# Seven half products for the last expert's first layer, set between the steps of two other experts

## The chip, the cores and the metric

The kernel runs on one core of a Trainium2 chip. The metric is the device time of one execution in microseconds (us). Executions of this kernel mostly agree within 0.3%, so a difference of 1 us in 385 is just within reach if a kernel is run five or six times. The profile also gives the span from the first to the last instruction, mostly 1.6 to 2.0 us shorter than the device time, and the mean granted clock of TensorE (1.0 is full speed).

I write PE for TensorE's matmuls, PEld for its weight loads, DVE for VectorE, ACT for ScalarE, POOL for GpSimd, SP for the engine whose queue issues most transfers. L12 is line 12 of the kernel that ran; a line has another number in another kernel. A bank is one of the buffers of 128x512 f32 in PSUM that a step of matmuls fills and ScalarE or VectorE empties.

## The reference

Attention over 4 batches of 768 positions and 8 heads makes the rows x. A mixture of four experts follows, and it is the part that matters here:

```python
# N, D, E, F = 3072, 512, 4, 1024
p = domain_probs / (domain_probs.sum(-1, keepdims=True) + 1e-09)
out = np.zeros((N, D))
for e in range(E):
    h = np.maximum(x @ w1[e], 0.0)          # first layer
    out += p[:, e:e + 1] * (h @ w2[e])      # second layer
```

## The kernel before

The first four tiles of 128 tokens are computed plainly: three together in a stage of "units", then one in a single-tile stage. The other twenty go in ten pairs. For a pair, each expert's inputs are scaled by its probability on VectorE (`scale_inputs`), the first layer is 32 matmuls over 256 columns (two tiles) per expert, and ScalarE evicts them with a Relu into blocks of `hA`. The second layer is already a Winograd-Strassen product: seven half products in place of eight, for which VectorE makes sums of the blocks (S1 to S4) and, once, sums of the weights (`tsb`).

```python
    blocks = hA.rearrange("p (b k x) -> p b k x", b=6, k=KT)
    A11, A21, A12, A22, S1, S2 = (blocks[:, n, :, :] for n in range(6))
    S3, S4 = A21, A12
    # ... cut ...
    def scale_inputs(nt0, e):
        xs = xs_of[0][:, e % 2, :, :]                    # two slots
        # ... out=o (xs), in0=x, in1=probabilities, on VectorE ...

    def input_sums(k0, k1):                              # VectorE
        # S1 = A21 + A22, S3 = A11 - A21, S2 = S1 - A11, for k0..k1

    def pair_steps(nt0, nxt):
        sums = [lambda: last_weight_sum(E - 1)] if nt0 == pair0 else []
        for e in range(E):
            if e + 1 < E:
                scale_inputs(nt0, e + 1)
            # ... load_probs(nxt) with the last expert ...
            for f0 in range(0, FTP, 2):                  # 4 steps of 8 matmuls
                # 8 matmuls of 256 columns -> one bank; Relu by ScalarE -> hA
                if sums:
                    sums.pop(0)()                        # one sum behind each step
                yield 2 * DMP * mm_ns(PC), 0.5
            # ... sums += input_sums(...) ...
        for op in sums:
            op()
        o = moe.tile([P, PT, DM], FP32, name="o", bufs=1)        # the outputs
        s = moe.tile([P, 3, HN], FP32, name="s", tag="sums", bufs=1)
        # ... seven products x, y in turn; store(0) after the sixth, store(1) after the seventh ...

    def moe_steps():
        # ... units ...
        for e in range(E):                               # the single tile
            yield from plain_steps(3, 1, e, ...)
            if e + 1 < E:
                last_weight_sum(e)
            if e == E - 3:
                scale_inputs(pairs[0], 0)
        for n, nt0 in enumerate(pairs):
            yield from pair_steps(nt0, ...)
```

Between the steps (at each `yield`) pieces of the attention of later chunks are put in, so every engine's queue mixes the two. The order in each queue is fixed when the kernel is built.

The softmax here doesn't subtract the row's maximum and nothing guards it: scores larger than these inputs give would overflow.

## Time and profile before

| | before |
|---|---|
| time, median of 3 | 384.93 us (384.45 to 385.48) |
| span of the profiled run, clock | 382.6 us, 0.999 |
| PE / DVE / ACT busy | 374.2 / 235.5 / 233.6 us |

The page gives busy time per engine over the span, then 40 slices of the span with the busy share in tenths. The view of stretches gives the same for any window. A busy share is an average, while a wait is decided by the one thing that comes last. And PE's idle time is counted from the modelled end of the last matmul, some 0.16 us after the next could have started (a matmul over 256 columns is given 272 ns, where one follows the other after 109), so short waits do not show at all and longer ones look a little too short.

### The profile page before, as it was taken

To read this page: it belongs to the slowest core of one execution; us is meant where nothing else is said; L and a number is where in the kernel's file an instruction comes from. 1 tells how busy PE (TensorE), PEld (TensorE's weight loads), DVE (VectorE), ACT (ScalarE), POOL (GpSimd) and SP (SyncE) were. 2 spreads that over 40 slices of the span, in tenths; PEclk is the share of its full clock that TensorE was granted. 3 is DMA by queue.
4 is the path that set the end of the run, shared out by engine and by line. 5 is a ranking of instruction groups with operands and counts; after the bars stand their busy time and mean duration, and the time that the engine had idled before them with its cause. 6 is when DMAs were issued, how large, how long until landed. Compare 5 with 4: busy or idle time off the path is not lost.

```text
span 382.6 us, 9369 instructions
## 1 busy us (share of the span) xinstructions
PE 374.2 (98%) x3814; PEld 312.2 (82%) x3814; DVE 235.5 (62%) x516; ACT 233.6 (61%) x476; POOL 111.7 (29%) x152
## 2 busy tenths in 40 slices
PE   8989999999999999999999999999999999999996
PEld 4755556577998898999888998899888999888885
DVE  7745787577866757766547567775556565345440
ACT  3863567657786876765765784674765684551630
POOL 8933644855138028113800118212100000000000
PEclk9999999999999999999999999999999999999999
DMA  9999999999499959974940759965510210110001
GB/s 165 150 207 201 185 174 193 149 159 177 67 139 130 123 101 96 143 134 50 138 72 20 123 102 82 151 123 38 81 55 15 67 57 2 57 56 30 29 0 57
DMA packets 127192, 39.19 MB, mean 102 GB/s; under 512 B 116232, under 2 KB 120876, under 8 KB 127148
## 3 DMA queue, kind: packets, MB, share of 16 engines
q0 software_dynamic: 86816, 19.01, 58.1%
q1 hardware_dynamic: 38732, 19.18, 22.3%
q8 instruction: 30, 0.49, 0.5%
q10 hardware_dynamic: 1600, 0.39, 0.5%
q14 instruction: 14, 0.11, 0.1%
HBM read 44.88 MB, written 6.34 MB: 134 GB/s over the span
## 4 chain that ended last, share of the span: by engine, by line
PE 86%; DMA 7%; POOL 3%; DVE 2%; ACT 1%; issue 0%; POOLq 0%; ACTq 0%
PE pA L1077 36%; PE pO L1110 32%; DMA w2sb<-in_moe_w_dram 7%; PE pO L986 5%; PE pA L639 5%; PE pA L965 4%; PE pV L687 2%; PE pV L751 2%; POOL vS L297 1%; ACT es L657 1%; POOL vR L291 1%; DVE kS L277 0%; POOL early L436 0%; DVE hA L1002 0%; POOL w1sb L322 0%
## 5 line engine op out<-in xcount | busy, mean ns | idle before, releaser
L1077 PE MATMUL pA<-xs,w1sb 128*128 128x256 f16 x1280 | 148.1, 272 | 0.1
L1077 PEld LDWEIGHTS <-w1sb 128*128 128x128 f16 x1280 | 122.5, 98 | 14.4 <-DVE xs L1043 0.4
L1086 ACT ACTIVATE hA<-pA 128x512 f16<-128x512 f32 x160 | 94.3, 597 | 39.2 <-PE pA L1077 36.7
L1110 PEld LDWEIGHTS <-hA 128*128 128x128 f16 x1120 | 106.6, 98 | 12.9
L657 ACT ACTIVATE es<-pA 128x384 f16<-128x384 f32 (+2 forms) x122 | 59.3, 510 | 32.4 <-PE pA L639 27.8
L1110 PE MATMUL pO<-w2sb,hA 128*128 128x256 f16 x640 | 77.8, 272 | 0.0
L293 POOL DMA_DIRECT2D vS<-in_v_dram x30 | 29.6, 988 | 124.5 <-PE pV L751 123.6
L1043 DVE TENSOR_TENSOR xs<-xT,pB 128x1024 f16<-128x1024 f16 (+1 forms) x52 | 49.6, 973 | 20.0 <-PE pA L1077 19.9
L1110 PE MATMUL pO<-tsb,hA 128*128 128x256 f16 x480 | 58.6, 272 | 0.0
L934 DVE TENSOR_TENSOR hA<-hA 128x1024 f16<-128x1024 f16 (+1 forms) x80 | 42.0, 553 | 1.1
L774 DVE TENSOR_TENSOR xT<-pV,rc 64x384 f16<-64x384 f32 x37 | 20.6, 556 | 25.9 <-ACT rc L779 23.8
L978 ACT ACTIVATE hA<-pA 128x384 f16<-128x384 f32 (+1 forms) x64 | 22.3, 386 | 20.3 <-PE pA L965 17.8
L965 PE MATMUL pA<-xT,w1sb 128*128 128x384 f16 (+1 forms) x256 | 31.7, 273 | 0.1
L986 PE MATMUL pO<-w2sb,hA 128*128 128x512 f16 x128 | 30.5, 379 | 0.3 <-DMA w2sb<-in_moe_w_dram 0.3
L1051 DVE TENSOR_TENSOR hA<-hA 128x512 f16<-128x512 f16 (+1 forms) x30 | 15.3, 512 | 18.8 <-ACT hA L1086 18.5
L769 ACT ACTIVATE rc<-pV,eps 64x384 f32<-64x384 f32 x37 | 21.3, 576 | 8.9 <-PE pV L751 7.7
L965 PEld LDWEIGHTS <-w1sb 128*128 128x128 f16 x256 | 19.3, 98 | 8.4 <-issue 0.5
L1131 DVE TENSOR_TENSOR o<-pO,s 128x256 f32<-128x256 f32 x30 | 12.7, 423 | 20.4 <-PE pO L1110 15.3
L639 PE MATMUL pA<-qT,kR 128*128 128x384 f16 (+2 forms) x120 | 23.3, 278 | 0.6 <-ACT qT L550 0.4
L1128 ACT COPY s<-pO 128x256 f32<-128x256 f32 x30 | 11.2, 373 | 18.1 <-PE pO L1110 17.3
L986 PEld LDWEIGHTS <-hA 128*128 128x128 f16 x128 | 11.9, 98 | 12.2 <-issue 0.5
L291 POOL DMA_DIRECT2D vR<-in_v_dram x24 | 19.0, 811 | 5.5 <-DMA w2sb<-in_moe_w_dram 4.0
(115 smaller groups left out, 331.7 us busy)
## 6 DMA issues: line engine op xcount, KB each, us to landing
pB<-p_rows SPq DMA_DIRECT2D x10, 512.0 KB, 3.6
out_dram<-o SPq DMA_DIRECT2D x19, 256.0 KB, 4.9
w1sb<-in_moe_w_dram POOLq DMA_DIRECT2D x8, 512.0 KB, 10.1
w2sb<-in_moe_w_dram POOLq DMA_DIRECT2D x4, 1024.0 KB, 13.2
vS<-in_v_dram POOLq DMA_DIRECT2D x30, 112.0 KB, 3.5
k_rows<-in_k_dram POOLq DMA_DIRECT2D x18, 128.0 KB, 4.4
q<-in_q_dram POOLq DMA_DIRECT2D x18, 128.0 KB, 5.7
vR<-in_v_dram POOLq DMA_DIRECT2D x24, 48.0 KB, 5.3
```

What stands on the lines that cost most here:

```text
L291: gp.dma_start(out=t[:, :, 0:D], in_=rows_of(v, b, h, c))
L293: gp.dma_start(out=t[:, :, own_v(h)], in_=windows_of(v, b, h, c))
L639: nc.tensor.matmul(out=ps[:, o : o + nq], lhsT=key_tile(b, c, h, t), rhs=qTs[b, c][:, hp, q0 : q0 + nq], start=(n == 0 or not first), stop ...
L657: nc.scalar.activation(out=es[:, 0:cols], in_=ps[:, 0:cols], func=AF.Exp, scale=SC)
L934: nc.vector.tensor_tensor(out=out, in0=a, in1=b, op=ALU.subtract)
L965: nc.tensor.matmul(out=pss[ft][:, 0:cols_n], lhsT=w1sb[:, e * DMP + ct, ft * P : (ft + 1) * P], rhs=x[:, ct, :], start=(n == 0), stop=(n = ...
L978: nc.scalar.activation(out=hs[:, ft, :], in_=ps[:, 0:cols_n], func=AF.Relu)
L986: nc.tensor.matmul(out=ps_o, lhsT=hs[:, ft, j * P : (j + 1) * P], rhs=w2sb[:, e * FTP + ft, :], start=(ft == 0), stop=(ft == FTP - 1),)
L1043: nc.vector.tensor_tensor(out=o, in0=xin, in1=pb.to_broadcast([P, DMP, n, P]), op=ALU.mult)
L1077: nc.tensor.matmul(out=ps[:, f * PC : (f + 1) * PC], lhsT=w1sb[:, e * DMP + ct, (f0 + f) * P : (f0 + f + 1) * P], rhs=xs[:, ct, :], start= ...
L1086: nc.scalar.activation(out=blocks[:, b0 : b0 + 2, k0 : k0 + 2, :].rearrange("p t f x -> p f t x"), in_=ps.rearrange("p (f t x) -> p f t x" ...
L1110: nc.tensor.matmul(out=ps, lhsT=a[:, k, :], rhs=b(k), start=(first and k == 0), stop=(k == KT - 1), skip_group_check=not first,)
```

## The change

Intent: PE is the bound, so do less on it. The last expert's first layer, over two tiles and both halves of its 512 inputs and 1024 outputs, is also a 2 x 2 product of blocks, so seven half products can take the place of eight. The products stand between the steps of experts 1 and 2, so that each of the two banks that they use has time to be emptied. Sums of w1 (`t1sb`) are made once; their room comes from dropping the block S2 (it now overwrites A11 after the first product of the second layer).

```diff
-    hA = pers.tile([P, 6 * KT * P], FP16, name="hA")
+    t1sb = pers.tile([P, 3, KH, FN], FP16, name="t1sb")
+    hA = pers.tile([P, 5 * KT * P], FP16, name="hA")
 ...
-    S3, S4 = A21, A12
+    S2, S3, S4 = A11, A21, A12
 ...
+    def first_weight_sums():
+        t = [t1sb[:, n, :, :] for n in range(3)]
+        return [
+            lambda: minus(t[0], w1_part(0, 1), w1_part(0, 0)),
+            lambda: minus(t[1], w1_part(1, 1), t[0]),
+            lambda: minus(t[2], w1_part(1, 0), t[1]),
+            lambda: minus(w1_part(0, 1), w1_part(1, 1), w1_part(0, 1)),
+        ]
 ...
+        def winograd_layer1():
+            s = moe.tile([P, 3, HN], FP32, name="s1", tag="sums", bufs=1)
+            o = moe.tile([P, PT, DM], FP32, name="o1", tag="o", bufs=1)
+            kept = [s..., o[:, 0, :], o[:, 1, :]]
 ...
+            product(x, w1_part(0, 0), x_part(0, 0), True)     # 8 matmuls of 128 columns
+            keep(0, x)                                        # ScalarE copy
+            yield ns, 0.5
+            product(y, w1_part(1, 0), x_part(0, 1), True)
+            add(0, y, 0)                                      # VectorE: add out of PSUM, then max
+            yield ns, 0.5
+            product(x, t(1), x_sum(1), False)
+            keep(1, x)
+            yield ns, 0.5
+            product(y, t(0), x_sum(0), True)
+            keep(2, y)
+            minus(x_part(0, 1), x_part(0, 1), x_sum(1))
 ...                                                          # three more products
+        scale_inputs(nt0, 1)
+        sums += [lambda: scale_inputs(nt0, EW)]               # EW: the last expert
+        if nt0 == pair0:
+            sums += [lambda: last_weight_sum(E - 1)]
+        sums += scaled_sums()
+        yield from plain_layer1(0)
+        products = winograd_layer1()
+        for e in (1, 2):
 ...
+            for step in plain_layer1(e):
+                yield step
+                step = next(products, None)
+                if step is not None:
+                    yield step
 ...
             if e == E - 3:
                 scale_inputs(pairs[0], 0)
+        for op in first_weight_sums():
+            op()
         for n, nt0 in enumerate(pairs):
```

More of the change, by code (lines that the diff above doesn't have):

```diff
@@ L109 @@
     tsb = pers.tile([P, 3, KT, HN], FP16, name="tsb")
-    hA = pers.tile([P, 6 * KT * P], FP16, name="hA")
+    EW = E - 1
+    KH, FN = DMP // 2, F // 2
+    t1sb = pers.tile([P, 3, KH, FN], FP16, name="t1sb")
+    hA = pers.tile([P, 5 * KT * P], FP16, name="hA")
     kR = []
@@ L126 @@
     ident16 = pers.tile([P, P], FP16, name="ident16")
-    early = moe.tile([P, 2528], FP16, name="early", tag="xs", bufs=1)
+    XS = 3 * DMP * 2 * P
+    early = moe.tile([P, XS + 2 * KH * P], FP16, name="early", tag="xs", bufs=1)
     warm = early[:, 1024:1536]
@@ L918 @@
     hA16 = hA
-    blocks = hA.rearrange("p (b k x) -> p b k x", b=6, k=KT)
-    A11, A21, A12, A22, S1, S2 = (blocks[:, n, :, :] for n in range(6))
-    S3, S4 = A21, A12
+    blocks = hA.rearrange("p (b k x) -> p b k x", b=5, k=KT)
+    A11, A21, A12, A22, S1 = (blocks[:, n, :, :] for n in range(5))
+    S2, S3, S4 = A11, A21, A12
     def whole_b(k, n, e, ft):
@@ L940, in weight_sums, with w1_part @@
         minus(t_rows(2, e), b_rows(1, 0, e), t_rows(1, e))
+    def w1_part(j, k):
+        return w1sb[:, EW * DMP + j * KH : EW * DMP + (j + 1) * KH, k * FN : (k + 1) * FN]
+    def first_weight_sums():
[6 more added lines that the diff above has]
+        ]
     def last_weight_sum(e):
@@ L948, in acc_of @@
     def acc_of(nt):
-        n0 = 2 * FTP * CH + nt * 2 * DM if nt < 3 else 6 * KT * P - 2 * DM
+        n0 = 2 * FTP * CH + nt * 2 * DM if nt < 3 else 5 * KT * P - 2 * DM
         return hA[:, n0 : n0 + 2 * DM].bitcast(FP32)
@@ L1030, in load_probs, with scaled @@
         )
+    def scaled(e):
+        n = 2 if e == EW else e % 2
+        x = xs_of[0][:, n * DMP * PC : (n + 1) * DMP * PC]
+        return x.rearrange("p (c x) -> p c x", c=DMP)
     def scale_inputs(nt0, e):
         if xs_of[0] is None:
-            xs_of[0] = moe.tile([P, 2, DMP, PC], FP16, name="xs", tag="xs", bufs=1)
-        xs = xs_of[0][:, e % 2, :, :]
+            xs_of[0] = moe.tile([P, XS + 2 * KH * P], FP16, name="xs", tag="xs", bufs=1)
+        xs = scaled(e)
         for g, c0, t0, n in pieces(nt0):
@@ L1057, in input_sums @@
             lambda: minus(S3[:, k, :], A11[:, k, :], A21[:, k, :]),
-            lambda: minus(S2[:, k, :], S1[:, k, :], A11[:, k, :]),
         ]
@@ L1064, in pair_steps, with step_done, plain_layer1 @@
     def pair_steps(nt0, nxt):
-        sums = [lambda: last_weight_sum(E - 1)] if nt0 == pair0 else []
-        for e in range(E):
-            if e + 1 < E:
-                scale_inputs(nt0, e + 1)
-            if e == E - 1 and nxt is not None:
-                load_probs(nxt)
-            xs = xs_of[0][:, e % 2, :, :]
+        sums = []
+        def step_done():
+            if sums:
+                sums.pop(0)()
+        def plain_layer1(e):
+            xs = scaled(e)
             for f0 in range(0, FTP, 2):
@@ L1092, in pair_steps, with x_part, x_sum @@
                 )
-                if sums:
-                    sums.pop(0)()
+                step_done()
                 yield 2 * DMP * mm_ns(PC), 0.5
-            if e == 1:
-                sums += input_sums(0, 2 * HT)
-            elif e > 1:
-                sums += input_sums(e * HT, (e + 1) * HT)
+        def x_part(i, j):
+            return scaled(EW)[:, j * KH : (j + 1) * KH, i * P : (i + 1) * P]
+        def x_sum(n):
+            x = xs_of[0][:, XS + n * KH * P : XS + (n + 1) * KH * P]
+            return x.rearrange("p (c x) -> p c x", c=KH)
@@ new lines, in scaled_sums, with s1, product, keep @@
+        def scaled_sums():
+            def s1():
+                nc.vector.tensor_tensor(
+                    out=x_sum(0), in0=x_part(1, 0), in1=x_part(1, 1), op=ALU.add
+                )
+            return [
+                s1,
+                lambda: minus(x_sum(1), x_sum(0), x_part(0, 0)),
+                lambda: minus(x_part(1, 0), x_part(0, 0), x_part(1, 0)),
+            ]
+        def winograd_layer1():
+            s = moe.tile([P, 3, HN], FP32, name="s1", tag="sums", bufs=1)
+            o = moe.tile([P, PT, DM], FP32, name="o1", tag="o", bufs=1)
+            kept = [
+                s.rearrange("p n x -> p (n x)")[:, 0 : HT * P], o[:, 0, :], o[:, 1, :]
+            ]
+            x = pO.tile([P, DM], FP32, name="pO", bufs=2)
+            y = pO.tile([P, DM], FP32, name="pO", bufs=2)
+            ns = HT * KH * mm_ns(P)
+            def product(ps, w, a, first):
+                for f in range(HT):
+                    for ct in range(KH):
+                        nc.tensor.matmul(
+                            out=ps[:, f * P : (f + 1) * P],
+                            lhsT=w[:, ct, f * P : (f + 1) * P],
+                            rhs=a[:, ct, :],
+                            start=(first and f == 0 and ct == 0),
+                            stop=(ct == KH - 1),
+                            skip_group_check=True,
+                        )
+            def keep(n, ps):
+                nc.scalar.copy(out=kept[n], in_=ps)
+            def block(n):
+                return blocks[:, n, EW * HT : (EW + 1) * HT, :]
+            def add(n, ps, b):
+                nc.vector.tensor_tensor(
+                    out=block(b),
+                    in0=ps.rearrange("p (f x) -> p f x", f=HT),
+                    in1=kept[n].rearrange("p (f x) -> p f x", f=HT),
+                    op=ALU.add,
+                )
+                nc.vector.tensor_scalar(
+                    out=block(b), in0=block(b), scalar1=0.0, scalar2=None, op0=ALU.max
+                )
+            def t(n):
+                return t1sb[:, n, :, :]
+            product(x, w1_part(0, 0), x_part(0, 0), True)
[10 more added lines that the diff above has]
+            minus(x_part(0, 1), x_part(0, 1), x_sum(1))
+            yield ns, 0.5
+            product(x, w1_part(0, 1), x_part(1, 0), False)
+            add(2, x, 3)
+            yield ns, 0.5
+            product(y, w1_part(1, 1), x_part(0, 1), False)
+            add(1, y, 2)
+            yield ns, 0.5
+            product(x, t(2), x_part(1, 1), False)
+            nc.scalar.activation(
+                out=block(1), in_=x.rearrange("p (f x) -> p f x", f=HT), func=AF.Relu
+            )
+            yield ns, 0.5
@@ new lines, in pair_steps @@
+        scale_inputs(nt0, 1)
[6 more added lines that the diff above has]
+        for e in (1, 2):
+            if e == 1:
+                scale_inputs(nt0, 2)
+            elif nxt is not None:
+                load_probs(nxt)
+            for step in plain_layer1(e):
[3 more added lines that the diff above has]
+                    yield step
+            sums += input_sums(0, 2 * HT) if e == 1 else input_sums(2 * HT, 4 * HT)
@@ L1138, in store, with second_sum @@
             nc.sync.dma_start(out=out[r, c], in_=o[:, i, c])
+        def second_sum(n):
+            k = slice(n * KT // 2, (n + 1) * KT // 2)
+            minus(S2[:, k, :], S1[:, k, :], A11[:, k, :])
         def fourth_sum(n):
@@ L1147, in pair_steps @@
         keep(0, x)
+        second_sum(0)
+        second_sum(1)
         yield half
@@ L1187, in moe_steps @@
         for e in range(E):
-            n0 = 2 * FTP * CH + 3 * 2 * DM + (e % 2) * FTP * P
+            n0 = (e % 2) * FTP * P
             yield from plain_steps(3, 1, e, lambda: xT[1][:, :, 0:P], n0)
@@ L1216 @@
     ONE = E * (FTP * DMP * mm_ns(P) + FTP * mm_ns(DM))
-    PAIR = E * FTP * DMP * mm_ns(PC) + 7 * KT * mm_ns(HN)
+    PAIR = (E - 1) * FTP * DMP * mm_ns(PC) + 28 * FTP // 4 * mm_ns(P) + 7 * KT * mm_ns(HN)
     def att_ns(a):
```

## The prediction

> **What bounds the kernel now.** I read first the busy shares and the 40 slices of the page. They say which engine is the wall and where.
>
> ```profile
> PE 374.2 (98%) x3814; PEld 312.2 (82%) x3814; DVE 235.5 (62%) x516; ACT 233.6 (61%) x476; POOL 111.7 (29%) x152
> ...
> PE   8989999999999999999999999999999999999996
> ...
> DVE  7745787577866757766547567775556565345440
> ...
> PEclk9999999999999999999999999999999999999999
> ```
>
> TensorE (PE) is at 9 tenths in nearly every slice, at full clock: the kernel is bound by matmuls. The table by stretches counts PE busy for all 205 us between 122 and 327 us, so before the change the token pairs have no visible wait. It follows that PE time saved is time won, and that any new wait of PE is lost in full. VectorE (DVE) has room on average, but it is at 5 to 8 tenths in the pair stage.
>
> Then the chain of waits, for the pace of each kind of matmul where nothing else runs between. The columns are start, duration, engine, tile, line, count.
>
> ```profile
> 79.45 1.79 PE pA L965 x32
> ...
> 326.94 13.97 PE pA L1077 x128
> 340.91 12.23 PE pO L1110 x112
> ```
>
> A pair's first layer, 128 matmuls over 256 columns, takes 13.97 / 128 = 109.1 ns each. Matmuls over 128 columns, each with its own weights (the single token tile, L965), take 1.79 / 32 = 55.9 ns each. So half the width costs 51% of the time. This decides whether seven half products pay.
>
> Then the groups by form, for what VectorE and ScalarE will have to do. Columns behind the bar: busy us, mean ns of one.
>
> ```profile
> L1086 ACT ACTIVATE hA<-pA 128x512 f16<-128x512 f32 x160 | 94.3, 597 | 39.2 <-PE pA L1077 36.7 <-PE pV L687 0.8
> L1043 DVE TENSOR_TENSOR xs<-xT,pB 128x1024 f16<-128x1024 f16 x28 | 34.2, 1220 | 14.2 <-PE pA L1077 14.0
> L934 DVE TENSOR_TENSOR hA<-hA 128x1024 f16<-128x1024 f16 x40 | 26.5, 688 | 0.5
> L934 DVE TENSOR_TENSOR hA<-hA 128x512 f16<-128x512 f16 x40 | 15.5, 419 | 0.6
> L998 DVE TENSOR_SCALAR hA<-pO,p_sb 128x512 f32<-128x512 f32 x4 | 3.0, 751 | 6.1 <-PE pO L986 6.1
> ```
>
> Last, the timeline at the start of the first pair (first group below) and that of the store queue at the end of the fourth pair.
>
> ```profile
> 93.88 1.22 DVE L1043 TENSOR_TENSOR xs<-xT,pB 128x1024 f16<-128x1024 f16 x1
> 95.02 0.69 DVE L934 TENSOR_TENSOR w2sb<-w2sb 128x1024 f16<-128x1024 f16 x1
> 95.15 0.77 PEld L1077 LDWEIGHTS <-w1sb 128*128 128x128 f16 x8 [0.39 <-DVE xs L1043]
> ```
>
> ```profile
> 209.49 0.33 SPq L1138 DMA_DIRECT2D out_dram<-o  x1
> 209.87 3.85 SPq L250 DMA_TRANSPOSE kT<-k_rows  x3
> 213.81 4.30 SPq L250 DMA_TRANSPOSE qT<-q  x3
> 218.20 0.53 SPq L1138 DMA_DIRECT2D out_dram<-o  x1
> ```
>
> The first shows that even now PE waits 0.39 us for expert 1's scaled inputs: VectorE is without a gap from 90.56 us to there, so anything put ahead of that scaling delays PE. The second shows that one of the two output stores of a pair sits behind six transposes, 8.7 us after the other, and 6.9 us after that pair's last matmul (211.3). Today nobody minds.
>
> **What the Trainium skill says.** "TensorE: Matmul & The Clock Gate", Back-to-back issue gap, gives a sustained 81 ns for a matmul of 128 columns in a stream of loads and matmuls, and 56 ns by its isolated formula N/2.4 + 2.5. This trace has 55.9 and 109.1 ns, both the formula; I use the trace. The same page (Architectural detail) calls ScalarE and VectorE strict first-in first-out: my waits below rest on that, and the timelines of the trace show no reordering. "VectorE: DVE Perf Modes", The perf-mode tier table, gives a two-tensor operation double rate from 16-bit SBUF and single rate with any PSUM operand. The trace agrees roughly: 1024 f16 elements in 688 ns, 512 f32 elements from PSUM in 751 ns. "DMA: Bandwidth & Descriptors" has about 2 us as a transfer's fixed cost; the trace's output stores take 4.0 to 5.8 us from issue to landing, and I use 4.9, the median.
>
> **The change, part by part.** There are ten pairs.
>
> PE. Removed per pair: one expert's 32 matmuls of 256 columns, 32 x 109.1 = 3.49 us. Added: 7 products of 4 x 2 matmuls of 128 columns, 56 x 55.9 = 3.13 us. Gain 0.36 us a pair, **3.6 us** in all, 0.9% of the time. Nothing else on PE changes. This is the ceiling.
>
> ScalarE. Four evictions of 597 ns go; three copies and one Relu of the same 128x512 come. No change.
>
> VectorE. Input sums per pair before: three of 1024 and six of 512 elements, 3 x 0.688 + 6 x 0.42 = 4.6 us; after, with S2 in S1-S3 halves, six of 1024, 4.1 us. Added: three additions out of PSUM (estimate 0.75 each, as L998), three max (estimate 0.28, the 128x480 tensor-scalar of L873 takes 0.279), four sums of 256 elements (estimate 0.285: 419 less 256 x 0.525, the slope between the two L934 forms). That is 3.1 + 1.1 - 0.5 = 3.7 us more a pair, and once 4 weight sums of some 0.7 = 2.8 us. VectorE goes from 235 to about 275 us, some 72%. In a pair without attention the slack holds: S1, S3 and the first half of S2 end some 2.6 us after the second layer begins (Relu 0.63, then three of about 0.65), and the third product, at 3.5 us, needs them.
>
> Where it does not hold:
> (1) First pair. The order of instructions puts the four weight sums just ahead of expert 1's scaling, that is at 93.88 us. It ends at 93.88 + 2.8 + 1.2 = 97.9 instead of 95.1, and PE waits **2.8 us** more.
> (2) The backlog goes on. From 93.88 up to the first addition out of PSUM, VectorE has 2.8 sums, 3 scalings 3.7, weight sum 0.7, three small sums 0.9, attention (two normalisations, three masks) 2.4, addition 0.75: 11.2 us, so 105.1. The fourth product, which reuses that bank, could start after 4 steps of 0.87, 3 products of 0.45 and four attention pieces of 0.18 from 97.9, plus 0.15 for the other scaling: 103.6. Wait **1.4 us**.
> (3) The products keep their sums in the buffer of the outputs, so the second copy must wait until both stores of the previous pair have landed. Usually store 2 lands 5.5 us into the pair and the copy comes at 3.5 + 3 x (0.87 + 0.45) = 7.4. In the fifth pair the store lands at 218.2 + 4.9 = 223.1; the copy is ready at 211.7 + 7.4 + 0.5 of attention = 219.6. ScalarE stands still for 3.5 us; PE runs on through a step, a product and a step (2.2 us) and then waits until 223.7, **1.8 us**. With the evictions piled up behind, I put 2.1.
> (4) Scattered: in-order VectorE at 80% in eight pairs with attention, 0.1 us a pair: 0.8 us.
>
> Sum: -3.6 + 2.8 + 1.4 + 2.1 + 0.8 = +3.5, that is 388.4. Waits that I may have overcounted (2 and 3 are differences of long sums) move my centre to 387.6.
>
> **The rivals.**
> A: the gain comes through and the waits are hidden. For it: 0.36 us a pair is in the trace, and products are interleaved to leave 2.2 us for each bank. Against: the sums ahead of a scaling that PE already waits for. Time: 381 to 383.
> B: TensorE pays more for narrow matmuls between wide ones, the skill's 81 ns: 56 x 81 = 4.54 us, 1.05 a pair more than now, 10 us slower with the waits on top, 395 to 400. Against: runs of 32 at 55.9 ns, followed by wide ones without a gap at 81.24 us.
> C: VectorE becomes the bound in pairs with attention. For it: 0.66 to 0.70 busy there now, about 0.80 after, in order, with waits of its own. Against: the last pairs, and slack of one to two microseconds at each hand-over. Each pair would lose 0.5 to 1 us: 390 to 393.
>
> **Range and chances.** Time 387.6 us. The low end, 383.5, is the gain with only (1) and little else; the high end, 391.5, is all waits plus half of C. Faster by over 2% would need 377.2, more than twice the ceiling: 0.01. Slower by over 2% is 392.6, B or a full C: 0.05. Within 2%: 0.94.
>
> **What would show it.** Right: narrow matmuls at 55 to 57 ns apart; the last two pairs each some 0.36 us shorter (25.85 instead of 26.2); PE idle of about 3 us at 95 to 98 us, ended by the scaling; a further wait of the fourth product for VectorE; in the fifth pair a ScalarE copy ended by a store; VectorE at 70 to 74%. Wrong: narrow matmuls at 65 ns or more (B); no idle PE in the first pair (1 and 2 fall, A); many PE waits for VectorE spread over all pairs (C); the copy in the fifth pair not held up (3 falls).

A word on reading it: "with S2 in S1-S3 halves" stands for two sums of 1024 elements for each of S1, S2 and S3; the wait in (2) is 105.1 less 103.6, which is 1.5 and not 1.4, and that in (3) is 223.7 less 221.8, 1.9 and not 1.8. The 751 ns held against the skill's two-tensor rate belong to an operation with one tensor (L998).

## The result, and the profile after

The changed kernel took 387.18 us (median of six, 386.50 to 389.27) against 385.01 for the kernel before in the same rounds. The ratio, which is the mean of the one kernel's fast runs over the mean of the other's in the same rounds and so not quite the ratio of these medians, is 1.0065 (95% interval 1.0041 to 1.0089). It is slower by 0.65%, "the same" at a threshold of 2%.

The page of the changed kernel, the lines that answer to those of the prediction:

```profile
PE 371.1 (97%) x4054; PEld 311.4 (81%) x4054; DVE 268.7 (70%) x590; ACT 229.5 (60%) x476; POOL 111.9 (29%) x152
...
PE   7889999999799999999999999999999999999996
```

PE has 3.1 us less work and still the span grew from 382.6 to 384.3. One slice, from 96 to 106 us, fell to 7 tenths: that is the first pair. VectorE went from 235.5 to 268.7 us.

Where is the time? The view of stretches, one line for each pair from its first matmul to that of the next (some boundaries lie 0.16 us late, at the modelled end of the matmul before, so sums of neighbouring pairs are safer than single ones). First the kernel before, pairs 1 to 5, 9 and 10 (length of the stretch, then busy us and count for PE, PEld, DVE, ACT and POOL, then the clock):

```profile
90.92:121.95 31.03, 30.92 (x360) 27.54 (x359) 23.05 (x55) 22.61 (x43) 11.91 (x14) 1.00 1.10 112
121.95:152.71 30.76, 30.76 (x358) 27.43 (x357) 21.90 (x51) 23.15 (x45) 11.84 (x14) 1.00 1.12 111
152.71:181.19 28.48, 28.48 (x325) 25.76 (x323) 19.76 (x48) 18.17 (x35) 5.95 (x7) 1.00 0.77 106
181.19:211.72 30.53, 30.53 (x329) 27.15 (x327) 17.83 (x41) 19.65 (x37) 8.53 (x10) 1.00 0.77 89
211.72:240.26 28.54, 28.54 (x307) 25.53 (x306) 17.74 (x37) 19.09 (x37) 11.50 (x13) 1.00 0.89 96
...
326.94:353.14 26.20, 26.20 (x242) 23.48 (x241) 11.67 (x20) 11.04 (x20) 0.00 (x0) 1.00 0.12 42
353.14:379.35 26.21, 26.20 (x240) 23.23 (x238) 9.19 (x16) 11.04 (x20) 0.00 (x0) 1.00 0.06 22
```

And the changed kernel, the same pairs:

```profile
91.16:125.17 34.01, 30.95 (x386) 27.75 (x384) 28.56 (x67) 22.64 (x44) 11.48 (x14) 1.00 0.95 102
125.17:155.94 30.77, 30.71 (x387) 27.45 (x384) 24.63 (x58) 23.12 (x46) 12.57 (x15) 1.00 1.20 114
155.94:184.64 28.70, 28.44 (x355) 25.79 (x352) 22.86 (x56) 17.43 (x35) 5.14 (x6) 1.00 0.73 100
184.64:214.46 29.82, 29.82 (x345) 26.81 (x342) 20.56 (x47) 18.74 (x37) 8.53 (x10) 1.00 0.75 89
214.46:243.97 29.51, 29.02 (x343) 25.91 (x340) 21.58 (x47) 19.40 (x39) 12.57 (x14) 1.00 1.00 102
...
329.36:355.19 25.83, 25.83 (x266) 23.48 (x265) 15.04 (x28) 10.58 (x20) 0.00 (x0) 1.00 0.12 42
355.19:381.04 25.85, 25.84 (x265) 23.24 (x262) 12.42 (x23) 10.58 (x20) 0.00 (x0) 1.00 0.06 21
```

The last two pairs, where no attention is mixed in, show the gain bare: 0.37 and 0.36 us each. The first pair became 2.98 us longer instead of 0.36 shorter, a loss of 3.3. Pairs 4 and 5 are taken together because attention moved from one to the other: 59.07 before, 59.33 after, where 58.35 was due, a loss of 1.0. Pairs 2 and 3 together took 59.24 before and 59.47 after, where 58.52 was due: a loss of 0.95.

The first pair in the timeline of the changed kernel (start and duration in us, engine, line, operation, out<-in, form, count; in brackets how long the engine was idle, and for what):

```profile
94.12 0.69 DVE L939 TENSOR_TENSOR t1sb<-w1sb 128x1024 f16<-128x1024 f16 x1
...
94.85 1.42 DVE L939 TENSOR_TENSOR t1sb<-w1sb,t1sb 128x1024 f16<-128x1024 f16 x2
...
96.18 0.68 DVE L939 TENSOR_TENSOR w1sb<-w1sb 128x1024 f16<-128x1024 f16 x1
96.78 2.35 DVE L1066 TENSOR_TENSOR xs<-xT,pB 128x1024 f16<-128x1024 f16 x2
...
98.06 1.05 PE L1100 MATMUL pA<-xs,w1sb 128*128 128x256 f16 x8 [2.77 <-DVE xs L1066]
...
103.41 0.68 DVE L1168 TENSOR_TENSOR hA<-pO,s 128x512 f16<-128x512 f32 x1
...
104.15 0.61 PE L1152 MATMUL pO<-xs,t1sb 128*128 128x128 f16 x8 [0.30 <-DVE hA L1168]
```

The four weight sums stand ahead of the scalings (L1066), and PE waits 2.77 us for the first of these. Then the fourth product waits 0.30 us more for the addition that empties its bank. Before the change the same step waited 0.39 us.

The store queue and the copy that waits for it, at the seam of pairs 4 and 5:

```profile
212.58 0.33 SPq L1262 DMA_DIRECT2D out_dram<-o  x1
...
212.97 3.85 SPq L255 DMA_TRANSPOSE kT<-k_rows  x3
...
216.91 3.83 SPq L255 DMA_TRANSPOSE qT<-q  x3
...
220.84 0.53 SPq L1262 DMA_DIRECT2D out_dram<-o  x1
...
224.50 0.59 ACT L1162 COPY o<-pO 128x512 f32<-128x512 f32 x1 [1.84 <-DMA out_dram<-o]
```

Store 1 is issued 8.3 us after store 0, behind six transposes, and ScalarE stands still for 1.84 us until it has landed.

### The profile page after: what moved, and what is told of

It reads as the page before. It is cut to its first block, busy times and chain, and to the rows that moved or that the text cites.

```text
span 384.3 us, 9934 instructions
## 1 busy us (share of the span) xinstructions
PE 371.1 (97%) x4054; PEld 311.4 (81%) x4054; DVE 268.7 (70%) x590; ACT 229.5 (60%) x476; POOL 111.9 (29%) x152
## 4 chain that ended last, share of the span: by engine, by line
PE 79%; DMA 8%; DVE 6%; POOL 3%; ACT 2%; issue 1%; POOLq 0%; ACTq 0%
PE pO L1234 32%; PE pA L1100 23%; PE pO L1152 7%; DMA w2sb<-in_moe_w_dram 7%; PE pO L1004 5%; PE pA L644 5%; PE pA L983 4%; PE pV L756 2%; PE pV L692 2%; DVE xs L1066 1%; DMA out_dram<-o 1%; POOL vS L302 1%; ACT es L662 1%; DVE kS L282 1%; POOL vR L296 1%
## 5 line engine op out<-in xcount | busy, mean ns | idle before, releaser
L1100 PE MATMUL pA<-xs,w1sb 128*128 128x256 f16 x960 | 120.0, 273 | 3.0 <-DVE xs L1066 3.0
L1100 PEld LDWEIGHTS <-w1sb 128*128 128x128 f16 x960 | 89.8, 98 | 12.8 <-DVE xs L1066 3.6
L1109 ACT ACTIVATE hA<-pA 128x512 f16<-128x512 f32 x120 | 71.1, 597 | 40.9 <-PE pA L1100 38.9
L1066 DVE TENSOR_TENSOR xs<-xT,pB 128x1024 f16<-128x1024 f16 (+1 forms) x52 | 48.7, 972 | 4.2 <-PE pA L1100 4.2
L939 DVE TENSOR_TENSOR hA<-hA 128x1024 f16<-128x1024 f16 x60 | 39.7, 686 | 0.6
L983 PEld LDWEIGHTS <-w1sb 128*128 128x128 f16 x256 | 19.3, 98 | 8.4 <-issue 0.5
L666 DVE TENSOR_TENSOR es<-es,mS 128x384 f16<-128x384 f16 (+1 forms) x40 | 13.6, 345 | 15.8 <-ACT es L662 15.6
L1152 PE MATMUL pO<-xs,w1sb 128*128 128x128 f16 x320 | 24.4, 219 | 0.1
L1074 DVE TENSOR_TENSOR hA<-hA 128x1024 f16<-128x1024 f16 x20 | 13.8, 689 | 12.7 <-ACT hA L1109 12.5
```

What stands on the lines that cost most here:

```text
L939: nc.vector.tensor_tensor(out=out, in0=a, in1=b, op=ALU.subtract)
L983: nc.tensor.matmul(out=pss[ft][:, 0:cols_n], lhsT=w1sb[:, e * DMP + ct, ft * P : (ft + 1) * P], rhs=x[:, ct, :], start=(n == 0), stop=(n = ...
L1066: nc.vector.tensor_tensor(out=o, in0=xin, in1=pb.to_broadcast([P, DMP, n, P]), op=ALU.mult)
L1100: nc.tensor.matmul(out=ps[:, f * PC : (f + 1) * PC], lhsT=w1sb[:, e * DMP + ct, (f0 + f) * P : (f0 + f + 1) * P], rhs=xs[:, ct, :], start= ...
L1109: nc.scalar.activation(out=blocks[:, b0 : b0 + 2, k0 : k0 + 2, :].rearrange("p t f x -> p f t x"), in_=ps.rearrange("p (f t x) -> p f t x" ...
L1152: nc.tensor.matmul(out=ps[:, f * P : (f + 1) * P], lhsT=w[:, ct, f * P : (f + 1) * P], rhs=a[:, ct, :], start=(first and f == 0 and ct == ...
```

## The experiments

Two batches of four kernels, each kernel four to six times in rounds with the kernel before, each batch on one chip. All gave correct results. Ratios are to the kernel before of the same batch.

| run | what | median us | ratio (95%) | granted clock of its runs |
|---|---|---|---|---|
| kernel before | first batch / second batch | 384.93 / 384.88 | 1 | 1.0 or 0.999 in 18 of 22, else 0.994 to 0.996 |
| e1_twice | three weight sums done twice | 390.77 | 1.0143 (1.0114 to 1.0173) | 0.987 to 0.995 |
| e2_reorder | weight sums behind the scalings | 386.03 | 1.0027 (1.0003 to 1.0051) | 0.998 to 1.0 |
| e3_early | three sums earlier | 384.05 | 0.9977 (0.9955 to 1.0000) | 0.998 to 1.0 |
| e4_keepbuf | kept sums not in the output buffer | 386.10 | 1.0029 (1.0004 to 1.0053) | 0.996 in four, 0.999 in one |
| e5_after_again | the changed kernel | 387.26 | 1.0059 (1.0039 to 1.0080) | 0.991 to 0.998 |
| e6_filler | idle matmuls in the wait | 386.29 | 1.0035 (1.0018 to 1.0052) | 1.0 in three, 0.996 in three |
| e7_best | all once-only sums out of the way | 382.99 | 0.9953 (0.9936 to 0.9970) | 0.999 to 1.0, one 0.996 |
| e8_best_keepbuf | e7 and e4 together | 381.93 | 0.9918 (0.9904 to 0.9932) | 1.0, one 0.996 |

### e1_twice: is it VectorE's work at that place?

```diff
-        for op in first_weight_sums():
+        for op in first_weight_sums()[:3] + first_weight_sums():
```

> The first three weight sums are done twice at their place ahead of expert 1's scaling, so 3 x 0.70 = 2.1 us more VectorE work there and nowhere else. My theory (VectorE's backlog at the first pair holds TensorE): the wait for the scaling grows from 2.8 to some 4.9 us, the time from 387.2 to 389.3. Rival (the loss is not there; it is the narrow matmuls or VectorE's load spread over all pairs): no visible change, 387.2 within 0.4.

The wait for the scaling grew from 2.77 to 4.82 us, so by the 2.05 us of the added sums. The backlog theory holds and its rival (loss elsewhere) falls. But the time grew by 3.6 us over the changed kernel's 387.18 (3.0 by the two ratios), not by 2.1. The timeline gives the first step after the wait 1.89 us for eight matmuls, where it takes 1.04 elsewhere, and the clock from 100 to 102 us, which holds most of it, is 0.50. Something other than the wait itself was being paid.

### e2_reorder: order, or the sum of the work?

```diff
         scale_inputs(nt0, 1)
-        sums += [lambda: scale_inputs(nt0, EW)]
+        if nt0 == pair0:
+            scale_inputs(nt0, EW)
+            for op in first_weight_sums():
+                op()
+        else:
+            sums += [lambda: scale_inputs(nt0, EW)]
```

(The call in front of the pairs is taken out.)

> The same four weight sums, but behind the scalings of experts 1 and 3 instead of ahead of them. Theory A (what counts is the order, the scaling was held up): the 2.8 us wait goes away, 384.4. Theory B, mine (what counts is all the VectorE work up to the first addition out of PSUM, which the fourth product needs): the wait moves from the scaling to the third and fourth products, which still begin at about 104 us in the profile, and the time stays at 387.2 within 0.4.

The timeline of this run, PE's waits in the first pair, which began at 92.33 us:

```profile
96.64 1.05 PE L1100 MATMUL pA<-xs,w1sb 128*128 128x256 f16 x8 [0.18 <-DVE xs L1066]
...
101.70 0.63 PE L692 MATMUL pV<-vR,es 128*128 128x65 f16 x6 [0.95 <-DVE x_one L712]
...
105.38 0.61 PE L1152 MATMUL pO<-xs,t1sb 128*128 128x128 f16 x8 [1.47 <-DVE hA L1168]
```

The wait for the scaling is down to 0.18 us and came back in two pieces, one of them at an attention matmul that I had not named. The fourth product starts 105.38 - 92.33 = 13.05 us into the pair; in the changed kernel it was 104.15 - 91.16 = 12.99. So order alone gains nothing there: what counts is all of VectorE's work up to that addition (theory B). Yet the time is 386.03, 1.2 us under the changed kernel, neither A's 384.4 nor B's 387.2. All six runs had a clock of 0.998 or more, while four of the changed kernel's first six had 0.995 or less. Their spans have a mean of 384.3 us; the changed kernel's three executions at 0.998 or 0.999 (e5, below) have 384.5, so at full clock the two orders cost the same. That made a new theory: one long stop of PE costs clock, three short ones do not (e6 shows that the second half of it does not hold everywhere).

### e3_early: three sums out of the way

```diff
             if e + 1 < E:
                 last_weight_sum(e)
+                first_weight_sums()[e]()         # in the single-tile stage
 ...
-            sums += [lambda: last_weight_sum(E - 1)]
+            sums += [first_weight_sums()[3], lambda: last_weight_sum(E - 1)]
```

> Three of the four weight sums go into VectorE's gaps of the single-tile stage, some 10 us earlier; the fourth stays between the scalings and the first addition. Theory B: 2.1 us of backlog less, the fourth product starts 2.1 us earlier (102 instead of 104.15), time 385.1; the wait for the scaling is gone but about 1 us of wait is left at the third or fourth product. Theory A: all of the wait goes, 384.4. Rival (the loss lies elsewhere): 387.2.

The fourth product starts 102.78 - 91.86 = 10.92 us into the pair, 2.07 earlier, as expected to within 0.1; 0.66 us of wait is left at the third. The time, 384.05, is a microsecond better than expected, and again all clocks are 0.998 or more.

### e4_keepbuf: the copy that waits for a store

```diff
-            o = moe.tile([P, PT, DM], FP32, name="o1", tag="o", bufs=1)
-            kept = [s.rearrange(...)[:, 0 : HT * P], o[:, 0, :], o[:, 1, :]]
+            s = s.rearrange("p n x -> p (n x)")[:, 0 : HT * P]
+            kept = [s, hA[:, 9 * KT * P // 2 : 5 * KT * P].bitcast(FP32), s]
```

The second half of S1 is free until the first layer is done, and the first kept sum has been used when the third comes.

> The kept sums of the seven products go into a free block of the sums and into the scratch of the second layer, no longer into the output buffer, so no copy waits for the stores of the pair before. My theory: in the fifth pair the 1.84 us wait of ScalarE for the store is gone and with it about 1.0 us of time (pairs four and five together were 1.0 us longer than expected): 386.2. Rival (ScalarE's wait is hidden): 387.2 within 0.3.

386.10, 1.1 us under the changed kernel; no engine waits for an output store any more, and PE has no wait in the fifth pair. Pairs 4 and 5 together take 58.34 us in its profile, where 58.35 was due. Four of its five runs have a clock of 0.996, so the 1.1 is hardly owed to the clock; e8 confirms it.

### e5_after_again: the clock of each execution

No edit.

> The changed kernel itself once more, as the measure for the runs of this call and to see the granted clock of each execution. New theory beside the backlog (from the clocks of the runs so far: 0.999 where the first pair's wait cost only itself, 0.995 and less where the clock stood at half for some 3.5 us after that wait): most executions have 0.991 to 0.996 and spans of 385 to 386, those with 0.999 have 384.3; median 387.2. Rival (the clock has nothing to do with it): spans do not go with the clock.

387.26, as in the first measurement. With both measurements there are twelve executions. Three at 0.998 or 0.999 have spans of 383.7 to 385.5, mean 384.5; six at 0.995 or 0.996 have 384.7 to 386.1, mean 385.2; three at 0.991 have 386.2 to 386.7, mean 386.4. On average the spans go with the clock, though the first two groups overlap. The expectation was too narrow at both ends (383.7 and 386.7), and two of the three fast-clock runs are off its 384.3.

This time the profile caught it. The stretches of e5 in the first pair; the last numbers are clock, share of the transfer engines, and GB/s:

```profile
96.00:98.00 2.00, 0.00 (x0) 0.00 (x0) 2.00 (x4) 0.00 (x0) 0.00 (x0) 1.00 0.00 0
98.00:100.00 2.00, 1.99 (x23) 1.91 (x24) 1.93 (x5) 0.60 (x1) 0.00 (x0) 0.75 0.00 0
100.00:102.00 2.00, 2.00 (x17) 1.50 (x16) 2.00 (x6) 0.60 (x2) 0.00 (x0) 0.50 0.24 49
102.00:104.00 2.00, 2.00 (x33) 1.91 (x31) 1.93 (x7) 1.24 (x3) 0.00 (x0) 0.90 0.52 105
```

The same wait in the first profile of the changed kernel, for comparison:

```profile
98.00:100.00 2.00, 1.94 (x26) 1.82 (x27) 1.93 (x6) 0.76 (x2) 0.00 (x0) 1.00 0.00 0
100.00:102.00 2.00, 2.00 (x30) 1.86 (x28) 2.00 (x6) 1.40 (x3) 0.00 (x0) 1.00 0.24 49
```

The kernel and the wait are the same (2.76 and 2.77 us), but in e5 the clock stood at half for 1.0 + 2.0 + 0.4 = 3.4 us after it, and PE did 17 matmuls in the two microseconds in which it otherwise does 30. PE calls itself fully busy all the while. What this cost is read at the fourth product of e5, whose first pair began at 91.12 us:

```profile
105.20 0.61 PE L1152 MATMUL pO<-xs,t1sb 128*128 128x128 f16 x8
```

It starts 14.08 us into the pair, against 12.99 in the first profile, although it no longer waits for the addition: 1.09 us lost with the same kernel and the same wait.

This looks like the HAM clock gate of "TensorE: Matmul & The Clock Gate", Part 1: half clock after an idle window of some 3.4 us, until a busy one has passed, with windows that run freely, which would let it hit by chance. Half clock for 3.4 us agrees with this trace; an idle stretch of 3.4 us does not, as the stop here is shorter.

By the mean clocks most executions lost something of this kind. One stretch of 3.4 us at half clock in 385 gives a mean of 0.996 (my estimate), two give 0.991. In the kernels with a stop of 2.7 us or more in the first pair (the changed one, e1, e4) 17 of 21 executions have 0.996 or less; in all others of the two batches 9 of 52. No kept profile caught two such stretches, so where the second lay in the executions at 0.991 is not known.

### e6_filler: is it the clock?

```diff
         yield from plain_layer1(0)
+        if nt0 == pair0:
+            ps = bank()
+            for n in range(20):
+                nc.tensor.matmul(
+                    out=ps[:, 0:PC], lhsT=w1sb[:, 0, 0:P], rhs=scaled(0)[:, 0, :],
+                    start=True, stop=True,
+                )
```

> 20 matmuls of 256 columns without use (2.2 us of work) stand in the wait for expert 1's scaling, which is untouched. If the lowered clock after a wait of about 3 us costs time, all executions have 0.998 or more and the time falls from 387.2 to 386.0, though there is more work. If the wait is only a wait: 387.2, or a little more.

386.29, a microsecond less than the changed kernel in the same rounds, with 2.2 us more of useless matmuls on the engine that is the bound. The intervals of the two ratios overlap, so this run alone would not carry the point; it agrees with the 1.09 us read in e5. The wait for the scaling is 0.58 us in its profile and the addition still holds the fourth product for 0.29. Not all went as expected: three of six runs have 0.996. The profiled one of these has its slow stretch from 20.9 to 24.3 us, in the start of the kernel, and full clock in the first pair:

```profile
18.61 0.29 PE L692 MATMUL pV<-vR,es 128*128 128x65 f16 x4 [0.76 <-ACT es L662]
...
20.88 0.66 PE L756 MATMUL pO<-es,vS 128*128 128x160 f16 x4 [1.10 <-DMA vS<-in_v_dram]
```

```profile
21.00:22.00 1.00, 1.00 (x9) 0.94 (x9) 0.10 (x1) 0.42 (x1) 1.00 (x2) 0.50 1.24 207
```

Here it fell after two short stops. The kernel before shows such a clock in four of 22 runs too, so that part is not the change's. I hold that the clock's cost is shown; that the other two slow runs of e6 also lost it at the start is only likely.

### e7_best: nothing of the once-only work ahead of the addition

As e3, and in addition the fourth weight sum goes right behind the last first-layer matmul of the single tile, and the last second-layer weight sum behind the addition:

```diff
-            yield from plain_steps(3, 1, e, lambda: xT[1][:, :, 0:P], n0)
+            for n, step in enumerate(plain_steps(3, 1, e, lambda: xT[1][:, :, 0:P], n0)):
+                if e == EW and n == FTP - 1:
+                    first_weight_sums()[3]()
+                yield step
 ...
-        if nt0 == pair0:
-            sums += [lambda: last_weight_sum(E - 1)]
         sums += scaled_sums()
+        if nt0 == pair0:
+            sums += [lambda: None, lambda: None, lambda: last_weight_sum(E - 1)]
```

> Three weight sums in gaps of the single-tile stage, the fourth in the gap right after the last first-layer matmul that reads its operand, and the second-layer weight sum of the last expert behind the first addition out of PSUM. Nothing of the change's once-only work is then ahead of that addition. Backlog theory: the fourth product begins 9.9 to 10.3 us after the first pair (12.99 in the changed kernel, 10.9 with three sums moved), no wait over 0.5 us in the first pair, time 383.2. If 384.0 as with three sums moved: the rest of the backlog was not what held it.

The fourth product starts 102.23 - 92.36 = 9.87 us into the pair and waits for nothing, so I had the backlog right to a few hundredths. The time is 382.99, as expected.

### e8_best_keepbuf: both

> Both mends: the once-only sums out of the way, and no copy that waits for a store. If the two losses add up: 1.0 us less than the run with the sums alone, 382.3, and under the kernel before by 2.7 of the 3.6 us that the matmuls save. If the store's wait was hidden: as the run with the sums alone, 383.2.

381.93, 1.06 us less than e7: the two losses add up, and the store's wait was not hidden. This version is under both kernels, 2.95 us under the kernel before, so 0.65 of the 3.6 us that the matmuls save are still missing. The trace shows where: the second and third pair together take 59.48 us in it, as in the changed kernel (59.47), where 58.52 was due. Of these 0.95 us the view of waits shows 0.3, at the third pair's scaling. No run tried to take this loss away.

## Why the prediction was right or wrong

The time (387.6 foretold, 387.18 and 387.26 measured), the range and the class came out right, and most of the mechanism. Terms (2) and (3) were too large by some 2 us together, a cost of 1.0 us was missing, and 0.8 us had been taken off the sum by hand; that these nearly cancelled is luck. Step by step:

- **The gain, 3.6 us: right.** 0.36 and 0.37 us in the two bare pairs. The first layer of a bare pair runs from 329.36 to 342.97 us in the chain of the changed kernel, 13.61 us, which is 96 x 109.1 + 56 x 55.9 ns. Rival B (81 ns a narrow matmul) is dead.
- **(1) Weight sums ahead of the scaling, 2.8 us: right.** The step of expert 1 starts 6.90 us into the pair instead of 4.23, so 2.67. But the step's reason was only half right. It reads as if the order did it; e2 shows that another order moves the wait and does not remove it.
- **(2) The backlog at the fourth product, 1.4 us: right in kind, too large.** The trace shows 0.30; from the third product's start to the fourth's it is 1.96 us where e7 has 1.50, so 0.46. VectorE was done with the addition at 104.09 and not at 105.1: I added durations, 11.2 us from the first sum on, and the chain took 9.97. The durations in this trace add up to 11.0, but a run of some twenty operations is shorter than their sum, as the next mostly begins before the last one ends (two scalings of 1.22 in 2.35 us), on average 0.05 us.
- **(3) The store, 2.1 us: right in kind, too large.** ScalarE stood still for 1.84 us and not 3.5, mostly since the store landed after 3.6 us, not 4.9. Its cost is 1.0 us by the lengths of pairs 4 and 5, 1.1 by e4 and 1.06 by e8. PE did not stop in one piece, as I had put it: of that 1.0 us the wait view shows 0.37, before the first product of the second layer, and the rest is in stops too short to show.
- **(4) Scattered waits, 0.8 us: about right in sum, but in two pairs and not in eight.** Pairs 2 and 3 lost 0.95 us by their lengths, while their attention matmuls take the same 6.8 us (my estimate from their counts in the trace and the pace of each width). The view shows 0.26 of it at the third pair's scaling and 0.06 of idle PE in the second pair; from start to start of the matmuls it is 0.43 at that scaling and 0.50 in three stops at attention matmuls of the second pair, each of which comes right after an operation of VectorE has ended. So rival C came in these two pairs, at the low end of its 0.5 to 1 us each, and not in pairs 4 and 6 to 8. VectorE is at 70%, the foot of the 70 to 74 foretold.
- **Missing: the clock, some 1.0 us.** I took the cost of a wait to be its length. In the profiles of e1, e4 and e5 the long wait brought half clock, 3.4 us of it in each (in e1 and e4 begun just before the wait ended), and by the mean clocks so it did in most executions. That halves up to 3.4 us of work, 1.7 us, of which some comes back because a later wait shrinks: 1.09 us are left in e5's timeline, and the difference of e6 is 1.0. The profile before could not show it, as it has no such wait in that stage; the skill's page, which I had cited for another matter, tells of half clock after idle windows.

With measured terms: -3.6 + 2.7 + 0.5 + 1.0 + 0.9 + 1.0 = +2.5, against +2.2 and +2.4 measured.

## What to carry to other kernels

Where the wall is one engine without a gap, a saving on it is won only if no other engine's queue gets new work ahead of what the wall needs next; once-only work is best put where its engine has gaps, and the test for it is the time of the first hand-over that it can delay, not the engine's busy share. Reusing a buffer couples its new writer to its old reader, here a copy to a store that sat behind six transposes. And a stop of PE near 3 us may cost more than its length, here 1.1 us more. That short stops are safe is not shown: in e2 they cost no clock, in the start of e6 two of 0.76 and 1.10 us did. Last, stops too short for the view of waits can add up to a microsecond; lengths of whole stretches find them.

## What the Trainium skill lacked or had wrong

- "TensorE: Matmul & The Clock Gate", Back-to-back issue gap: its sustained 81 ns for a matmul of 128 columns in a stream with weight loads is not what this kernel shows. Runs of 32, each with its own weights, and the narrow products between wide steps run at 55.9 ns, wide ones of 256 columns at 109.1: both its isolated formula.
- The same page, Part 1: it asks for an idle window of about 3.4 us and advises against gaps over 3.4 us (over some 3 in its closing table). Here no length of one stop decides. The clock fell after stops of 2.76 us (as shown; some 2.9 with the modelled end taken off) in e4 and e5, after one of 2.44 us in the start of e8, and after two of 0.76 and 1.10 us in the start of e6. It did not fall after one of 2.77 us in the first profile of the changed kernel, nor after 2.63 us in the start of e7, nor after stops of up to 1.5 us in the first pair of e2 (six runs at 0.998 or more). PE is shown as fully busy while the clock is at half, so it is the clock column and the matmul count of a stretch that tell.
